# A hash-masked attention and MLP kernel: score banks, spare slots for exponentials, one way of hashing, weights in two transfers, and a new order

## The chip, the cores and the metric

The kernel runs on one core of a Trainium2 chip. The metric is the device time of one execution in microseconds (us). Three runs of the kernel before took 304.24 to 305.08 us, with a median of 304.82. A profile of one more execution (303.7 us) shows what each engine did; the profiled span, from the first to the last instruction of the program, is 302.0 us.

Engines: TensorE (PE; PEld is its loading of weights), VectorE (DVE), ScalarE (ACT), GpSimd (POOL) and SyncE (SP). SP's queue issues most DMAs, POOL's queue those that convert fp32 to bf16 on the way.

## The reference

The kernel computes attention in which a query sees only keys of its own hash bucket, and then a layer norm and an MLP with a residual. Shapes: q, k, v are (4, 8, 768, 64): 4 batches, 8 heads, 768 positions, 64 dimensions; proj is (64, 6); w_ch1 is (512, 2048) and w_ch2 (2048, 512); the result is (4, 768, 512).

```python
q_bits = (np.einsum('bhsd,dk->bhsk', q, proj) > 0)
k_bits = (np.einsum('bhsd,dk->bhsk', k, proj) > 0)
mask = q_bucket[:, :, :, None] == k_bucket[:, :, None, :]
scores = np.where(mask, 0.125 * np.matmul(q, k.transpose(0, 1, 3, 2)), -1e9)
attn = softmax(scores)
x = np.matmul(attn, v)                      # heads side by side: (4, 768, 512)
xn = (x - mean(x)) / sqrt(var(x) + 1e-6) * g_ln
out = x + relu(xn @ w_ch1) @ w_ch2
```

(The lines are shortened: the bucket is the number that the six bits form.)

## The kernel before

**Units and steps.** The 768 positions of each of 4 batches are cut into 3 blocks of 256 queries, so there are 12 units u. The 8 heads are two groups g of four heads. For a unit and a group, the 768 keys are taken in three parts kp of 256. So there are 72 steps s = 6u + 3g + kp, and each has three parts:

- S (line 516): 24 products. For each of two blocks of 128 keys and four heads, one product of the hash bits and two of the halves of the 64 dimensions add up in PSUM. Equal hashes add a constant that the exponential's bias takes away again; unequal ones end so far below that the exponential is 0.
- E (line 522): two exponentials on ScalarE, two heads each (128 x 1024 elements), from the score banks into an SBUF tile E.
- A (line 541): 16 products of E with the values v, with a column of ones that gives the denominator, into the accumulator `acc` of the unit and group.

After the three steps of a group come `na` and `nb` (the division, DVE), `nc` (statistics) and, after both groups, `ce` (mean away, times g_ln). The result is transposed (`ft`, `fc` with TensorE for unit 0, `fl` by DMA for the others). The MLP's first product is F (line 598): 8 pieces p for each unit, each 8 products over 256 columns of w1. R is its relu (DVE, line 608, or ACT, line 606). D (line 614) is the second product, Z (line 622) the residual, O the output DMA.

**Score banks.** PSUM has the tags scA, scB and acc, each of two banks, and f1, f2. The two halves of a step's scores go to scA and scB. For the steps named in `ROT` they rotate over scA, scB and acc instead, as `acc` holds nothing yet; A's accumulator has the tag acc, so the first A waits for the last exponential that reads scores from there.

**SBUF slots.** `SLOTS` gives each tile of a tag its buffer by hand. E has four buffers, `hb` (the relu's result) two, `x` (a unit's attention result) four.

**Batch 0's hash.** q and k of batch 0 come in pieces of 256 positions: `lx` (line 338) loads, `tn` (DVE, line 270) transposes twice, `ca` (lines 277 to 281) casts to bf16. The hash of a piece goes one of two ways. The full product: `ha` (line 359) is four fp32 products with the projection spread over all 128 columns (`pfull`), and `bh` (line 273) compares with 0 on DVE into the bit tile G. The compact way: `hc` (line 370) is 16 small products with `p32`, `bc` compares, `sl` (line 383) is four products with a matrix `spread` that brings the bits to their place, and `bi` (lines 393 to 395) copies them to G, on DVE or ACT. `sel` makes `spread` on POOL. Eight pieces go the first way and four the second. The other batches are loaded as a whole (`LX`, after a marker `gx` in the first column), transposed with `tu`, cast with `CA`, hashed with `hm` and spread by way of DRAM (`mw`, `mr`).

**Weights.** `lw1` loads a quarter of w1 (512 columns: F's pieces 2n and 2n+1), `lw2` a quarter of w2, `lg` (line 398) g_ln, copied to all partitions (`gB`). `lv` loads v (batch 0 in two loads of four heads), `cv` (POOL, line 417) casts it, `sq` and `sc` make its sum over keys. `wm` (line 331) are products that nothing reads; they keep TensorE busy at the start.

**Order.** `ORDER` is a hand-given list of operations, read once: a word is the operation, the engine (v DVE, a ACT, p POOL, s SP, t TensorE) and its arguments. Each engine does its own words in this order, and waits where data or a buffer isn't ready; so S.t.6.2 is step 6's S, F.t.0.1 unit 0's piece 1, and E.a.5.1 the second half of step 5's exponentials. The first steps come in the order 0, 1, 2, 4, 3, 5, 8, 6, 7, 9, 10.

Of the kernel before, what the change touches and what calls it, by code (L numbers as in the profile page):

```python
# [38 lines left out]
tu.v.1.1.0.0 A.t.12.2 E.a.13.1 LX.s.2.0.0 S.t.16.2 E.a.16.0 E.a.16.1 A.t.13.2 tu.v.1.1.1.3 tu.v.1.1.0.1 tu.v.1.1.0.3 rs.p.0
D.t.0.0.2 D.t.0.0.3 mr.s.1.0.1 cv.p.1.4.0 Z.v.0.0 tu.v.1.1.1.1 CA.p.1.1.1 cv.p.1.4.2 S.t.15.2 lv.s.1.0.2 cv.p.1.0.0 E.a.15.0  # L40
mr.s.1.0.2 mr.s.1.0.3 hm.t.1.1 E.a.15.1 D.t.0.1.0 CA.a.1.1.0 S.t.17.2 E.a.17.1 mr.s.1.0.0 bt.v.1.1 mw.s.1.1 mr.s.1.1.3
na.v.2.0 nb.v.2.0 F.t.1.2 R.v.1.2 su.p.1.0 A.t.15.2 E.a.17.0 cv.p.1.0.2 A.t.16.2 F.t.1.6 S.t.18.2 R.a.1.6
nc.v.2.0 F.t.1.5 R.v.1.5 D.t.0.1.1 mr.s.1.1.2 E.a.18.0 A.t.17.2 E.a.18.1 sp.t.1.0 sc.v.1.0 na.v.2.1 S.t.20.2
# [637 lines left out]
```

## Time and profile before

| what | time or share |
|---|---|
| runs | 304.24, 304.82, 305.08 us |
| profiled execution | 303.7 us, of it the span 302.0 us |
| F, 768 products (line 598) | 99.3 us busy, mean 273 ns |
| S, 1728 products (line 516) | 52.4 and 42.6 us busy |
| A, 1152 products (line 541) | 46.2 us busy |
| E, 144 exponentials (line 522) | 153.5 us busy, mean 1111 ns |
| first E begins | 10.00 us |
| first F begins on the chain of waits | 35.46 us |
| TensorE's last product ends | 298.3 us |
| DMA read and written | 28.12 MB and 6.88 MB |

Products on TensorE overlap, so busy times of single products are longer than the steps from one to the next; the chain of waits gives the latter (F's 8 products: 0.87 us; A's 16: 0.49; S's 24: 0.77 to 0.83). In the chain each row is a start, a duration, and the engine and line that the program's end hung on at that time. In a timeline a row is one or several instructions of one kind, with the idle time ahead of them in square brackets.

### The profile page before, as it was taken

What the parts mean: (1) busy time and instruction counts of PE and PEld (TensorE: products, weight loads), DVE (VectorE), ACT (ScalarE), POOL (GpSimd) and SP (SyncE); (2) the same over time, 40 slices, a digit from 0 to 9 for tenths busy, and PEclk for the clock granted to TensorE, in tenths of its full rate; (3) what the DMA queues carried; (4) which work ended last, traced back from release to release, by engine and by line L of the source; (5) the groups of instructions that cost most, each with busy time, mean ns of one, the idle gap of its engine ahead of it and who ended that gap; (6) DMA issues with size and microseconds to landing.
All of it is one profiled execution on the core that took longest, in us unless ns stands there. A gap on an engine that the chain in (4) does not pass through costs nothing.

```text
span 302.0 us, 9823 instructions
## 1 busy us (share of the span) xinstructions
PE 290.5 (96%) x4345; PEld 202.5 (67%) x4394; DVE 175.9 (58%) x364; ACT 189.0 (63%) x206; POOL 76.4 (25%) x103
## 2 busy tenths in 40 slices
PE   8988899999999999999999999999999999999995
PEld 4666677676766767677666776667666776676663
DVE  4878758759767564875749466274554346443322
ACT  2587888778646777777667866854565665643010
POOL 5497062476017101300750002700101001001000
PEclk9999999999999999999999999999999999999999
DMA  6999999718768453420322242012201501003132
GB/s 221 310 299 247 282 212 270 177 35 230 201 159 246 84 217 95 98 72 18 80 66 41 68 100 51 21 35 54 54 2 35 106 2 37 20 2 89 52 87 71
DMA packets 31194, 34.32 MB, mean 114 GB/s; under 512 B 15536, under 2 KB 27824, under 8 KB 31152
## 3 DMA queue, kind: packets, MB, share of 16 engines
q1 hardware_dynamic: 26080, 28.98, 35.0%
q0 software_dynamic: 4224, 4.19, 8.5%
q8 instruction: 34, 0.56, 0.8%
q10 hardware_dynamic: 848, 0.53, 0.7%
q14 instruction: 8, 0.07, 0.1%
HBM read 28.12 MB, written 6.88 MB: 116 GB/s over the span
## 4 chain that ended last, share of the span: by engine, by line
PE 94%; ACT 3%; issue 1%; DVE 0%
PE f L598 29%; PE sc L516 19%; PE acc L541 12%; PE hp L471 3%; ACT E L522 3%; PE hf L359 2%; PE warm L328 1%; PE f_110None L614 1%; PE f_101None L614 1%; PE f L614 1%; PE f_90None L614 1%; PE f_20None L614 1%; PE f_80None L614 1%; PE f_21None L614 1%; PE f_00None L614 1%
## 5 line engine op out<-in xcount | busy, mean ns | idle before, releaser
L522 ACT ACTIVATE E<-sc,bias_sb 128x1024 bf16<-128x1024 f32 x144 | 153.5, 1111 | 60.6 <-PE sc L516 60.6
L598 PE MATMUL f<-xnT,w_sb 128*128 128x256 bf16 x768 | 99.3, 273 | 0.1
L598 PEld LDWEIGHTS <-w_sb 128*128 128x128 bf16 x768 | 70.8, 98 | 22.6 <-issue 7.4
L608 DVE TENSOR_SCALAR hb<-f 128x512 bf16<-128x512 f32 x49 | 33.7, 690 | 59.2 <-PE f L598 58.8
L614 PEld LDWEIGHTS <-hb 128*128 128x128 bf16 x400 | 36.0, 98 | 31.2 <-issue 3.0
L516 PE MATMUL sc<-qb,kb 32*128 32x256 bf16 x1152 | 52.4, 267 | 0.0
L606 ACT ACTIVATE hb<-f 128x512 bf16<-128x512 f32 x47 | 28.0, 596 | 35.9 <-PE f L598 35.9
L541 PEld LDWEIGHTS <-E 128*128 128x128 bf16 x1152 | 42.7, 98 | 8.2 <-issue 3.2
L541 PE MATMUL acc<-vaug,E 128*128 128x65 bf16 x1152 | 46.2, 194 | 0.1
L516 PE MATMUL sc<-G 6*128 6x256 bf16 (+1 forms) x576 | 42.6, 273 | 2.7 <-ACT E L522 2.0
L576 POOL TENSOR_SCALAR rs<-mv 128x2 f32<-128x2 f32 x12 | 7.7, 640 | 106.9 <-DVE mv L570 106.6
L516 PEld LDWEIGHTS <-kb 32*128 32x128 bf16 x1152 | 30.4, 93 | 1.5
L516 PEld LDWEIGHTS <-G 6*128 6x128 bf16 (+1 forms) x576 | 15.7, 91 | 20.7 <-issue 17.4
L417 POOL CAST vaug<-vn 128x768 bf16<-128x768 f32 x16 | 14.0, 884 | 58.3 <-DMA vn<-in_v_dram 44.2
L270 DVE STREAM_TRANSPOSE T<-X 128x384 f32<-128x384 f32 (+2 forms) x52 | 26.8, 542 | 1.2 <-DMA X<-in_k_dram 1.2
L554 DVE SCALAR_TENSOR_TENSOR y<-vsB,acc 128x520 f32<-128x520 f32 x24 | 16.5, 688 | 10.5 <-PE acc L541 10.2
L571 DVE SCALAR_TENSOR_TENSOR xc<-x,mv,gB 128x512 bf16<-128x512 f32 x24 | 18.6, 775 | 0.9
L567 DVE BATCH_NORM_STATS2 st<-x 128x6 f32<-128x256 f32 x48 | 17.7, 412 | 0.3
L563 DVE TENSOR_TENSOR x<-y,rc 128x512 f32<-128x512 f32 x24 | 16.8, 699 | 0.8
L425 POOL TENSOR_TENSOR t<-vn 128x768 f32<-128x768 f32 x6 | 10.9, 1812 | 0.0
L281 POOL CAST kb<-T 128x1536 bf16<-128x1536 f32 x3 | 4.4, 1461 | 22.3 <-DVE T L270 22.3
L270 DVE STREAM_TRANSPOSE tp<-X 128x256 f32<-128x256 f32 x24 | 9.0, 416 | 1.4 <-DMA X<-in_q_dram 0.9
(113 smaller groups left out, 236.7 us busy)
## 6 DMA issues: line engine op xcount, KB each, us to landing
out_dram<-x SPq DMA_DIRECT2D x45, 128.0 KB, 2.0
X<-in_k_dram SPq DMA_DIRECT2D x7, 768.0 KB, 5.8
X<-in_q_dram SPq DMA_DIRECT2D x6, 768.0 KB, 4.7
vn<-in_v_dram SPq DMA_DIRECT2D x24, 192.0 KB, 6.0
w_sb<-in_moe_w_ch_dram POOLq DMA_DIRECT2D x8, 512.0 KB, 15.9
vn<-in_v_dram SPq DMA_DIRECT2D x2, 768.0 KB
X<-in_q_dram SPq DMA_DIRECT2D x2, 512.0 KB, 12.2
Bd<-B SPq DMA_DIRECT2D x6, 96.0 KB, 2.5
```

Of the source, the lines that this page charges most:

```text
L270: nc.vector.transpose(d[:, j], s[:, j, kj0 : kj0 + n])
L516: nc.tensor.matmul(sc(s, i // 2)[:, i % 2, 256 * kk : 256 * kk + 256], lh, rh, start=(rep == 0), stop=(rep == 2), skip_group_check=True,)
L522: nc.scalar.activation(E(s)[:, heads(h)], sc(s, h), AF.Exp, scale=EXP_SCALE, bias=bias_sb)
L541: nc.tensor.matmul(acc[:, qt, (D + 1) * i : (D + 1) * (i + 1)], E(s)[:, i, 256 * kk + P * qt : 256 * kk + P * qt + P], vaug(u // 3)[:, 4 * ...
L554: nc.vector.scalar_tensor_tensor(yt(u, g), vs, EPS_ROW, made[f"acc{u}{g}"][:, :, :A], op0=AOP.mult, op1=AOP.add,)
L563: nc.vector.tensor_tensor(xo, a[:, :, :, 0:D], rc.to_broadcast([P, 2, 4, D]), op=AOP.mult)
L567: nc.vector.bn_stats(stats(u)[:, qt, g], xt(u)[:, qt, 256 * g : 256 * g + 256])
L571: nc.vector.scalar_tensor_tensor(xc(u)[:, t], xt(u)[:, t], mv(u)[:, t, 0:1], gB, op0=AOP.subtract, op1=AOP.mult,)
L598: nc.tensor.matmul(f1[:, n].rearrange("p (t x) -> p t x", t=2), w1_sb[:, dt, P * nt : P * nt + P], xnT(u)[:, :, dt], start=(dt == 0), stop ...
L606: nc.scalar.activation(hb(u)[:, 2 * p : 2 * p + 2], f1, AF.Relu)
L608: eng.tensor_scalar_max(hb(u)[:, 2 * p : 2 * p + 2], f1, 0.0)
L614: nc.tensor.matmul(f2, hb(u)[:, nt, P * t : P * t + P], w2_sb[:, nt, half(h)], start=(nt == 0), stop=(nt == NNT - 1),)
```

## The change

Five edits come together. `ROT` names six steps instead of three, so the scores of steps 4, 3 and 5 rotate over three bank pairs too. The E tiles of the first four of these steps take the slots of hb (steps 0 and 1) and x (2 and 4). `sel`, `hc`, `Bc`, `bc`, `sl` and `bi` are gone, and all twelve pieces of batch 0 are hashed by `ha` and `bh`. `lw1` loads half of w1 (1024 columns: F's pieces 0 to 3 or 4 to 7), so there are two of them. The order is a new one: three `wm` instead of eight, `lg` second on SP's queue, three casts of queries on DVE, and, up to the first F, this:

```diff
-ROT = (0, 1, 2)
+ROT = (0, 1, 2, 4, 3, 5)
 ORDER = """
-mem.v lp.a lx.a.0.1.0.1 tab.a pf.v lx.s.0.0.0.1 warm.t wm.t.0 wm.t.1 wm.t.2 wm.t.3 sel.p
-tn.v.0.0.0 p32.p tn.v.0.1.0 ca.p.0.1.0 lx.s.0.1.1.3 ha.t.0.0.0 wm.t.4 lx.s.1.1.0.3 lx.s.1.0.0.1 ha.t.0.1.0 lv.s.0.0.4 ca.a.0.0.0
-lx.s.0.0.1.3 bh.v.0.0.0 wm.t.5 tn.v.0.1.1 ha.t.0.1.1 lw2.p.1 bh.v.0.1.0 ca.p.0.1.1 S.t.0.2 lv.s.0.4.4 E.a.0.0 E.a.0.1
-tn.v.0.1.2 tn.v.1.1.1 ca.p.1.1.1 lx.s.1.0.1.3 wm.t.6 wm.t.7 bh.v.0.1.1 ha.t.1.1.1 on.p.0 bh.v.1.1.1 tn.v.1.1.0 S.t.1.2
-E.a.1.0 ca.v.0.1.2 gx.p.1.0.0 ha.t.0.1.2 bh.v.0.1.2 E.a.1.1 tn.v.1.0.0 ca.p.1.0.0 ca.v.1.1.0 ha.t.1.1.0 bh.v.1.1.0 tn.v.1.1.2
-S.t.2.2 E.a.2.0 cv.p.0.0.0 ha.t.1.0.0 bh.v.1.0.0 S.t.4.2 cv.p.0.0.2 tn.v.0.0.1 hc.t.0.0.1 ca.p.0.0.1 lw1.p.3 bc.v.0.0.1
-gx.p.1.0.1 ha.t.1.1.2 LX.s.1.0.0 tn.v.0.0.2 E.a.2.1 E.a.4.0 LX.s.1.0.1 E.a.4.1 bh.v.1.1.2 sl.t.0.0.1 bi.v.0.0.1 cv.p.0.4.2
-A.t.0.2 S.t.3.2 A.t.1.2 ca.v.1.1.2 lg.s lw1.p.1 sq.t.0.0 E.a.3.0 A.t.2.2 sc.v.0.0 E.a.3.1 S.t.5.2
-E.a.5.0 cv.p.0.4.0 sq.t.0.4 na.v.0.0 nb.v.0.0 lw1.p.2 lw1.p.0 nc.v.0.0 E.a.5.1 S.t.8.2 sc.a.0.4 A.t.5.2
-E.a.8.0 E.a.8.1 tu.v.1.0.0.2 lw2.p.0 tn.v.1.0.1 A.t.4.2 ca.p.1.0.1 hc.t.0.0.2 tn.v.1.0.2 A.t.3.2 tu.v.1.0.1.0 bc.v.0.0.2
-lw2.p.3 gx.p.1.1.1 tu.v.1.0.0.1 sl.t.0.0.2 na.v.0.1 bi.a.0.0.2 S.t.6.2 E.a.6.0 LX.s.1.1.1 E.a.6.1 hc.t.1.0.1 nb.v.0.1
-hc.t.1.0.2 bc.v.1.0.2 sl.t.1.0.2 bi.a.1.0.2 bc.v.1.0.1 pmem.p S.t.7.2 A.t.8.2 E.a.7.0 lv.s.1.4.1 nc.v.0.1 ce.v.0.1
-ce.v.0.0 ft.t.0.1 lv.s.1.4.2 E.a.7.1 fc.a.0.1 sl.t.1.0.1 tu.v.1.0.1.1 bi.v.1.0.1 A.t.6.2 ft.t.0.0 S.t.9.2 E.a.9.0
-on.p.1 lw2.p.2 fc.v.0.0 E.a.9.1 F.t.0.6 F.t.0.7 tu.v.1.0.1.2 R.a.0.6 A.t.7.2 tu.v.1.0.0.0 S.t.10.2 R.v.0.7
-na.v.1.0 nb.v.1.0 lv.s.1.4.0 tu.v.1.0.0.3 tu.v.1.0.1.3 E.a.10.0 CA.p.1.0.1 F.t.0.3 F.t.0.4 E.a.10.1 A.t.9.2 ca.a.0.0.2
...
-O.s.10.0 R.v.11.2 D.t.11.0.0 F.t.11.5 R.a.11.5 O.s.10.2 D.t.11.0.1 F.t.11.7 O.s.10.3 D.t.11.0.2 R.v.11.7 D.t.11.0.3
-D.t.11.1.0.0 D.t.11.1.1.0 D.t.11.1.2.0 O.s.8.2 D.t.11.1.3.0 D.t.11.1.0.1 D.t.11.1.1.1 rs.p.11 Z.v.11.0 O.a.11.0.0 O.s.11.0.1 Z.v.11.1.0
-O.a.11.1.0.0 O.s.11.1.1.0 D.t.11.1.2.1 D.t.11.1.3.1 Z.v.11.1.1 O.s.11.1.1.1 O.a.11.1.0.1
+mem.v lp.a lx.a.0.1.0.1 tab.a pf.v pmem.p warm.t on.p.0 wm.t.0 lx.s.0.0.0.1 lg.s tn.v.0.0.0
+tn.v.0.1.0 ha.t.0.0.0 lx.s.0.1.1.3 bh.v.0.0.0 ha.t.0.1.0 lx.s.1.1.0.3 bh.v.0.1.0 ca.a.0.0.0 wm.t.1 wm.t.2 lx.s.1.0.0.1 tn.v.0.1.1
+ca.a.0.1.0 S.t.0.2 p32.p tn.v.0.1.2 on.p.1 ha.t.0.1.1 E.a.0.0 bh.v.0.1.1 tn.v.1.1.1 ha.t.0.1.2 ca.p.0.1.1 S.t.1.2
+gx.p.1.0.0 bh.v.0.1.2 tn.v.1.0.0 lx.s.0.0.1.3 E.a.0.1 ca.p.0.1.2 ca.p.1.1.1 lv.s.0.0.4 cv.p.0.0.0 E.a.1.0 cv.p.0.0.2 tn.v.1.1.0
+ha.t.1.1.1 bh.v.1.1.1 ca.v.1.1.0 S.t.2.2 lx.s.1.0.1.3 ca.v.1.0.0 ha.t.1.0.0 tn.v.0.0.1 E.a.1.1 E.a.2.0 lv.s.0.4.4 bh.v.1.0.0
+ha.t.1.1.0 tn.v.1.1.2 cv.p.0.4.2 bh.v.1.1.0 lw2.p.2 E.a.2.1 S.t.4.2 E.a.4.0 ha.t.1.1.2 E.a.4.1 S.t.3.2 E.a.3.0
+tn.v.0.0.2 ha.t.0.0.1 ca.v.1.1.2 gx.v.1.0.1 cv.p.0.4.0 tn.v.1.0.2 bh.v.1.1.2 ca.v.0.0.1 S.t.5.2 bh.v.0.0.1 ca.v.0.0.2 E.a.3.1
+tn.v.1.0.1 sq.t.0.0 sc.v.0.0 E.a.5.0 S.t.8.2 E.a.5.1 A.t.0.2 A.t.2.2 ca.p.1.0.2 E.a.8.0 LX.s.1.0.0 tu.v.1.0.0.1
+tu.v.1.0.0.2 gx.p.1.1.1 lv.s.1.4.0 A.t.1.2 na.v.0.0 sq.t.0.4 nb.v.0.0 nc.v.0.0 E.a.8.1 S.t.6.2 A.t.5.2 A.t.3.2
+A.t.4.2 sc.a.0.4 E.a.6.0 E.a.6.1 LX.s.1.0.1 tu.v.1.0.1.2 na.v.0.1 nb.v.0.1 lv.s.1.4.2 nc.v.0.1 lw1.p.1 ha.t.1.0.1
+S.t.7.2 E.a.7.0 bh.v.1.0.1 ha.t.1.0.2 bh.v.1.0.2 lv.s.1.4.3 ha.t.0.0.2 lv.s.1.0.3 ca.p.1.0.1 lw1.p.0 lw2.p.0 tu.v.1.0.0.3
+E.a.7.1 S.t.9.2 E.a.9.0 A.t.7.2 ce.v.0.1 bh.v.0.0.2 A.t.8.2 E.a.9.1 gx.v.1.1.0 lw2.p.1 ce.v.0.0 ft.t.0.0
+fc.v.0.0 A.t.6.2 na.v.1.0 tu.v.1.0.1.3 ft.t.0.1 LX.s.1.1.0 fc.a.0.1 rs.p.0 tu.v.1.0.1.0 S.t.10.2 E.a.10.0 tu.v.1.0.1.1
+F.t.0.6 tu.v.1.0.0.0 CA.p.1.0.0 A.t.9.2 LX.s.1.1.1 CA.v.1.0.1 E.a.10.1 R.a.0.6 F.t.0.7 S.t.11.2 E.a.11.0 E.a.11.1
+A.t.10.2 R.v.0.7 F.t.0.1 lv.s.1.0.2 R.v.0.1 F.t.0.4 R.a.0.4 S.t.14.2 E.a.14.0 F.t.0.3 lv.s.1.0.0 E.a.14.1
...
+R.a.11.5 O.s.9.1 O.s.10.2 rs.p.11 D.t.11.1.1.0 F.t.11.6 R.a.11.6 O.s.9.0 D.t.11.0.2 O.s.10.0 D.t.11.0.3 Z.v.11.0
+O.a.11.0.0 D.t.11.1.2.0 O.s.11.0.1 D.t.11.1.3.0 D.t.11.1.0.1 Z.v.11.1.0 O.a.11.1.0.0 O.s.11.1.1.0 D.t.11.1.1.1 D.t.11.1.2.1 D.t.11.1.3.1 Z.v.11.1.1
+O.a.11.1.0.1 O.s.10.3 O.s.11.1.1.1
 SLOTS = dict(
-    Bc="0120",
-    E="012301213021301230132031230120313210302103230123021320120302130212310230",
+    E="01231012301203123013210321020301230123031203123031210320123012031231",
...
-    X="0123021302310210",
-    hb="010101010101",
+    X="0123021320310230",
+    hb="01010101010101",
...
-    x="012301230123",
+    x="01230132013201",
...
     def E(s):
-        return sb(f"E{s}", [P, 4, 512], BF16, "E", 4)
+        tag, bufs = (("hb", 2), ("hb", 2), ("x", 4), ("x", 4))[ROT.index(s)] if s in ROT[:4] else ("E", 4)
+        return sb(f"{'E' if tag == 'E' else 'E' + tag[0]}{s}", [P, 4, 512], BF16, tag, bufs)
...
-    def sel(eng):
...
-    def hc(eng, g, t, kp):
...
-    def bc(eng, g, t, kp):
...
-    def sl(eng, g, t, kp):
...
-    def bi(eng, g, t, kp):
...
     def lw1(eng, n):
-        nc.gpsimd.dma_start(out=w1_sb[:, :, 512 * n : 512 * n + 512], in_=w1ap[:, :, 512 * n : 512 * n + 512])
+        nc.gpsimd.dma_start(out=w1_sb[:, :, 1024 * n : 1024 * n + 1024], in_=w1ap[:, :, 1024 * n : 1024 * n + 1024])
```

In the middle of the order, left out here, the same F, D, S and A of the later units are interleaved in another sequence.

More of the change, by code (lines that the diff above doesn't have):

```diff
@@ L39 @@
[L39 to L43, printed above, removed]
@@ new lines @@
+D.t.6.1.0 S.t.58.2 nb.v.8.1 nc.v.8.1 ce.v.8.1 F.t.7.4 E.a.58.0 su.p.3.4 R.a.7.4 E.a.58.1 ce.v.8.0 A.t.56.2
+D.t.6.1.1 fl.s.8.1 sp.t.3.4 sc.v.3.4 D.t.6.1.2 sp.t.3.0 sc.a.3.0 S.t.59.2 E.a.59.1 E.a.59.0 F.t.7.5 R.v.7.5
+A.t.55.2 D.t.6.1.3 Z.v.6.1 cv.p.3.4.2 F.t.7.3 O.s.5.2 R.v.7.3 S.t.60.2 E.a.60.0 E.a.60.1 O.s.5.0 na.v.9.0
+fl.s.8.0 D.t.7.0.0 F.t.8.5 R.a.8.5 nb.v.9.0 nc.v.9.0 A.t.58.2 S.t.61.2 F.t.7.6 E.a.61.0 A.t.57.2 R.a.7.6
+A.t.59.2 rs.p.8 F.t.8.3 na.v.9.1 O.s.6.0 E.a.61.1 R.v.8.3 S.t.64.2 E.a.64.0 E.a.64.1 D.t.7.0.1 O.s.6.1
@@ L297, in pmem @@
         )
-    def sel(eng):
-        nc.gpsimd.memset(spread, 0.0)
-        for c in range(CC):
-            nc.gpsimd.affine_select(
-                out=spread[:, c].rearrange("p (i b) -> p i b", b=32)[:, :, :NB],
-                in_=ones.rearrange("p (i b) -> p i b", b=32)[:, :, :NB],
-                pattern=[[-8, 4], [-1, NB]], base=-32 * c, channel_multiplier=1, compare_op=AOP.is_equal, fill=0.0,
-            )
     def tab(eng):
@@ L640 @@
     OPS = dict(
-        mem=mem, pmem=pmem, tab=tab, lp=lp, sel=sel, pf=pf, p32=p32c, warm=warm, wm=wm, lx=lx, tn=tn, ca=ca, ha=ha, bh=bh, hc=hc, bc=bc, sl=sl, bi=bi, lg=lg,
+        mem=mem, pmem=pmem, tab=tab, lp=lp, pf=pf, p32=p32c, warm=warm, wm=wm, lx=lx, tn=tn, ca=ca, ha=ha, bh=bh, lg=lg,
         lw1=lw1, lw2=lw2, on=on, lv=lv, cv=cv, su=su, sp=sp, sq=sq, sc=scp, LX=LX, gx=gx, tu=tu, CA=CA, hm=hm, bt=bt, mw=mw, mr=mr,
```

163 lines of the change are left out of this document (70 added, 93 removed).

## Prediction

> **What bounds the kernel now.** I read the page's busy shares first, then the busy times of six stretches, then the chain of waits up to 50 us, then VectorE (DVE), GpSimd (POOL) and SyncE (SP) in order of time.
>
> ```profile
> PE 290.5 (96%) x4345; PEld 202.5 (67%) x4394; DVE 175.9 (58%) x364; ACT 189.0 (63%) x206; POOL 76.4 (25%) x103
> ...
> 8.50:20.34 11.84, 11.26 (x185) 7.78 (x183) 9.86 (x26) 8.47 (x8) 8.14 (x12) 1.00 1.09 335
> 20.34:35.46 15.12, 12.57 (x313) 9.73 (x314) 12.00 (x31) 12.02 (x15) 8.12 (x14) 1.00 1.07 246
> 35.46:60.45 24.99, 24.63 (x450) 17.85 (x454) 16.70 (x35) 20.93 (x23) 9.58 (x8) 1.00 1.01 224
> 60.45:294.76 234.31, 231.15 (x3350) 160.96 (x3396) 131.23 (x252) 145.42 (x159) 46.04 (x55) 1.00 0.32 79
> ```
>
> The columns are the stretch, its length, then busy us of PE, PEld, DVE, ACT, POOL, the granted clock, DMA share and GB/s. From the first F (35.46) on TensorE is busy 98 to 99% of the time: whatever is still to be done then is done at its pace. Time can be won ahead of 35.46, where its work waits, and after its last matmul (298.3). So what counts is how much product work is done by the time the first F starts.
>
> ```profile
> 19.32 1.02 PE sc L516 x24
> 20.35 2.12 ACT E L522 x2
> 22.51 0.84 PE sc L516 x22
> 23.36 2.12 ACT E L522 x2
> 25.52 0.83 PE sc L516 x22
> ...
> 29.51 2.13 ACT E L522 x2
> 31.68 0.83 PE sc L516 x22
> ...
> 34.44 1.02 PE sc L516 x24
> 35.46 1.85 PE f L598 x16
> ```
>
> From 19 us the path alternates: 24 score products (S, 0.83), then two exponentials (E, 2.12), then the next S, which needs the bank pair that E has just read. That is a step every 3.0 us, though ScalarE needs 2.12. The three-bank rotation covers only steps 0, 1, 2.
>
> ```profile
> 13.57 0.76 DVE L270 STREAM_TRANSPOSE tp<-X 128x256 f32<-128x256 f32 x2
> 14.26 0.60 DVE L281 CAST kb<-tp 128x512 bf16<-128x512 f32 x1
> 14.79 0.41 DVE L273 TENSOR_SCALAR G<-hf 128x256 bf16<-128x256 f32 x1
> ...
> 19.43 1.18 DVE L281 CAST kb<-tp 128x512 bf16<-128x512 f32 x1
> ...
> 20.05 1.24 POOL L417 CAST vaug<-vn 128x768 bf16<-128x768 f32 x1
> ...
> 20.54 2.00 SPq L398 DMA_DIRECT2D gB<-in_moe_g_ln_dram  x1
> ```
>
> DVE feeds the early steps: a pair of transposes each 0.69 us after the one before (0.77 busy, overlapped), a hash comparison 0.35, a key cast 0.53. The last two rows are a cast and a load that the change moves or doubles.
>
> **The change, part by part.** I follow the new order on each engine with these durations.
>
> *Head.* Five of eight single warm-up products (L331) go; three of the first four (0.43 each) stand ahead of the first hash product, which ends at 7.04 now. It can start at 5.05 instead, partly at the slow rate of the warm-up (0.86 warm, 1.72 at half rate; I take 1.3). Both first hash products are then done at 7.15, step 0's S starts at 7.6 and its E at 8.5 instead of 10.00: 1.5 us earlier. SP issues gB (2.00) second, ahead of five X pieces and both v loads. Its 256 KB cost the keys between 0.8 (335 GB/s) and 2.0 (the issue); at the 232 GB/s of the first 8.5 us it is 1.1, and I take that: the last keys land near 10.2.
>
> *Hash by full products.* Four hc+sl pairs (0.36 + 0.12) become four ha (0.86): 4 x 0.38 = 1.5 us more TensorE work, all of it before the first F, where ScalarE's 2.12 a step covers it; uncovered it costs the 1.5. On DVE bc + bi (0.23 + 0.41) becomes one comparison (0.42). POOL loses `sel` (0.53 + 0.83), which nothing waits for. DVE makes five of batch 0's casts instead of three, three of them of queries: no row has that at this size; it lies between 0.32 (a third of the 0.96 of a 128x1536 one) and 0.62 (a key cast), or 1.18 where a POOL cast runs beside it. I take 0.5.
>
> *Third bank pair, E in hb and x slots.* With DVE's chain the E start at 8.5, 11.1, 13.2, 16.3 (step 4 waits for its query hash on DVE; 17.33 now), 18.4, 20.5, 22.65 (step 8; 26.35 now). From step 6 on the pairs alternate again, 3.1 each: 25.75, 28.95, 32.0, the last being step 9, done at 34.1; now step 7 ends at 34.58. A (the E-times-v products) start only when the accumulator bank is free of scores, at 22.65 instead of 18.84, and the second group's end near 27.2 instead of 28.4. The longer life of the first E costs nothing, as hb and x are first written after 24 us. Then the normalization (7.0 us from A to F now: 28.4 to 35.4) gives the transposed x at 34.4, step 10's S follows, and F starts at 35.25. Gain: 0.2 on the start, and one S (0.77) and one A (0.50) more are done by then: 1.27. Together 1.5.
>
> *Weights.* w1 comes in two transfers of 1024 columns. The third F (F.0.1, at 38.8) now needs the second of them; before, the quarter that it reads was used only at 47. Before, four quarters issued from 19.2 on; the last, issued at 23.5, landed 17.2 us later, at 40.7. Alone on the queues a 512 KB piece takes 2.5 us (212 GB/s between 40.7 and 45.7). Five pieces' worth (a quarter of w2 goes ahead) from 20.7 on is 12.4 us, and 1.5 MB of X and v in between is 3.9 at the 400 GB/s of 16 to 20 us: 37.0. Two more X loads, issued near 32, add up to 3.9: 41. So its wait lies between 0 and 2.2 us; those X loads need some 3.9 us from issue to first packet (20.16 to 24.06 for the same load now), so I take 38.5, no wait.
>
> [...]
>
> *Order anew.* Counting neighbours on TensorE after the first F and pricing each pair of kinds by its mean in this trace (an F after an A costs 0.97, after a D 0.91; an A after an F 0.61, after a D 0.51), the new order is 0.3 us cheaper, beside the S and A already counted. *Tail:* SP issues one more output (O.10.3) between the last two pieces, one issue of 0.44; 0.3 us later, between 0 and 0.5.
>
> **Sum:** -1.5 - 0.3 + 0.3 = -1.5. The profiled execution took 303.7 (span 302.0 and 1.7 around it), so 302.2; the median of the runs is 304.82, 1.1 above it, so **303.3**. Own bounds 302.2 to 304.2: the start of step 4 by 0.9 either way (casts at 0.32 or 0.62, gB at 0.8 or 2.0).
>
> **Rivals.**
> *The second half of w1 is late* (the slower side). F.0.1 stands on TensorE and holds F.0.4, S 14 and all behind them: with its landing at 41 to 43 the wait is 2.2 to 4.2, so 305.5 to 307.5. For it: four pieces needed 21.5 us from first issue to last landing, and from 35 us on X loads run beside the weights as before. Against: gB is out of the way and POOL issues the two as early as 23 and 25. It decides from a landing of 38.8 on.
> *DVE sets the pace of the first steps.* The banks are free but the hash comes late, from gB ahead of the keys (0.9 more) and casts at 1.18 (0.6 more each, two or three of five meeting POOL's four v casts). F starts 1.2 to 2.7 later: 304.5 to 306.0, the gain gone. For it: DVE is busy 9.86 of 11.84 us from 8.5 on. Against: from step 3 on it has 0.7 to 1.9 us in hand in my walk.
> [...]
> *More than I count.* No cost of gB, casts at 0.32, no tail: 301.7 to 302.2.
>
> **How the numbers follow.** A measurement of this kernel tells 0.3% (0.9 us) from no change: faster is under 303.9, slower over 305.7. The forecast has 0.50 (0.45 faster, 0.05 same), the weights 0.26 (0.25 slower, 0.01 same), DVE 0.16 (0.09 same, 0.07 slower), more gain 0.08 (faster): faster 0.53, same 0.15, slower 0.32. The range runs from 302.0 to 306.8; the likeliest case's own is 302.2 to 304.2.
>
> **What would show it.** Right: first E near 8.5, step 8's near 22.7, no idle ScalarE between steps 4, 3, 5, 8; first F within 0.5 us of 35.3 with eleven S and nine A ahead of it; TensorE waiting for no DMA. Wrong: TensorE idle ahead of F.0.1 until a w landing (the weights); E of step 4 after 17.3, or DVE casts over 1 us (DVE's pace); X from k landing after 11; idle TensorE after 60 us, which would be a fault of the new order that I have priced at nothing.

## The result, and the profile after

The changed kernel takes 310.12 us (median of six runs, 307.55 to 313.04) against 304.78 for the kernel before in the same measurement (304.24 to 305.08). Two of the six, 312.51 and 313.04, count as slow runs and are left out of the ratio; the other four have a median of 308.08. The ratio is 1.0136, with an interval of 1.0099 to 1.0174. It is slower by 1.4%, where 303.3 was forecast, in a range of 302.0 to 306.8. All six runs after spread over 5.5 us, those before over 0.8. The profiled execution took 308.59 us, with a span of 306.8.

The page's busy shares after, and the busy times of the stretches that were shown of before:

```profile
PE 292.9 (95%) x4279; PEld 202.8 (66%) x4325; DVE 175.5 (57%) x363; ACT 185.7 (61%) x204; POOL 83.3 (27%) x95
```

```profile
0.00:8.50 8.50, 5.18 (x14) 2.23 (x14) 2.81 (x17) 2.12 (x3) 1.97 (x14) 1.00 0.63 202
8.50:20.34 11.84, 11.48 (x123) 7.23 (x124) 9.21 (x25) 7.60 (x8) 5.88 (x8) 0.86 1.03 353
20.34:35.46 15.12, 14.09 (x250) 10.29 (x251) 12.35 (x30) 12.39 (x13) 7.85 (x9) 1.00 1.01 211
35.46:60.45 24.99, 23.83 (x455) 17.64 (x454) 19.21 (x39) 19.10 (x23) 11.85 (x8) 1.00 0.97 240
60.45:294.76 234.31, 230.56 (x3386) 160.48 (x3429) 130.19 (x252) 143.32 (x158) 55.80 (x57) 1.00 0.32 77
```

From 60 us on little has changed: TensorE is busy 230.56 us of it against 231.15, and one F waits 0.7 us for a transposed load. The loss lies ahead. Two numbers of the second row must be read together: TensorE is busy 11.48 us, more than before, but runs 123 products instead of 185 (of those missing, 20 are the compact hash's and 19 are A, which the new order has later), at a granted clock of 0.86. Busy is not fast. The head shows why, in VectorE's rows, TensorE's and SyncE's (start, duration, the idle time ahead in brackets). First the row of the first key piece before, then the rows after:

```profile
4.97 0.77 DVE L270 STREAM_TRANSPOSE tp<-X 128x256 f32<-128x256 f32 x2 [0.17 <-DMA X<-in_k_dram]
```

```profile
4.25 0.77 DVE L268 STREAM_TRANSPOSE tp<-X 128x256 f32<-128x256 f32 x2 [1.08 <-DMA X<-in_q_dram]
7.92 0.77 DVE L268 STREAM_TRANSPOSE tp<-X 128x256 f32<-128x256 f32 x2 [2.90 <-DMA X<-in_k_dram]
...
8.42 1.68 PE L348 MATMUL hf<-tp,pfull 128*128 128x256 f32 x4 [2.21 <-DVE tp L268]
...
1.57 0.59 SPq L357 DMA_DIRECT2D gB<-in_moe_g_ln_dram  x1
```

The first key piece is transposed at 7.92 instead of 4.97. TensorE idles 2.21 us for it and then takes 1.68 us for four products that take 1.13 at full clock (at 14.97 of the same trace): between 8.42 and 12.30 the granted clock is 0.56. From 4 to 5 and from 5 to 6 us, when the key piece should land and the next ones follow, the queues move 169 and 158 GB/s, where before they moved 350 and 325 (the last column; before, then after):

```profile
4.00:5.00 1.00, 1.00 (x4) 0.36 (x3) 0.80 (x3) 0.17 (x1) 0.00 (x0) 1.00 1.12 350
5.00:6.00 1.00, 1.00 (x4) 0.43 (x3) 0.74 (x2) 0.46 (x1) 0.12 (x1) 1.00 1.04 325
```

```profile
4.00:5.00 1.00, 1.00 (x4) 0.40 (x3) 0.75 (x2) 0.00 (x0) 0.00 (x0) 1.00 0.63 169
5.00:6.00 1.00, 1.00 (x5) 0.70 (x4) 0.02 (x1) 0.63 (x1) 0.00 (x0) 1.00 0.67 158
```

gB, issued at 1.57, is the only transfer that is new there. In the DMA records its 128 packets run from 3.82 to 7.32 us. The key piece's last packet ends at 7.38 (4.41 before), although its load was issued earlier, at 1.22, on ScalarE's queue.

ScalarE's rows, the first F's surroundings on TensorE, and the piece of w1 on the chain of waits:

```profile
12.39 2.12 ACT L481 ACTIVATE Eh<-sc,bias_sb 128x1024 bf16<-128x1024 f32 x2 [2.58 <-PE sc L475]
15.08 2.12 ACT L481 ACTIVATE Eh<-sc,bias_sb 128x1024 bf16<-128x1024 f32 x2 [0.57 <-PE sc L475]
17.09 2.12 ACT L481 ACTIVATE Ex<-sc,bias_sb 128x1024 bf16<-128x1024 f32 x2
20.07 2.12 ACT L481 ACTIVATE Ex<-sc,bias_sb 128x1024 bf16<-128x1024 f32 x2 [0.87 <-PE sc L475]
22.12 6.13 ACT L481 ACTIVATE E<-sc,bias_sb 128x1024 bf16<-128x1024 f32 x6
...
33.48 2.12 ACT L481 ACTIVATE E<-sc,bias_sb 128x1024 bf16<-128x1024 f32 x2 [1.96 <-PE sc L475]
```

```profile
32.55 0.29 PE L475 MATMUL sc<-G 32*128 32x256 bf16 x4 [0.67 <-issue]
44.07 1.92 PE L557 MATMUL f<-xnT,w_sb 128*128 128x256 bf16 x16 [0.79 <-DMA w_sb<-in_moe_w_ch_dram]
```

```profile
24.98 1.45 POOL qb L277
26.43 17.59 DMA w_sb<-in_moe_w_ch_dram
```

The third bank pair works: one row holds six exponentials (three steps) without a gap, and step 8 is done at 28.25 although the first E began at 12.39, 2.4 us later than before. S of step 7 waits 0.67 us for nothing that the profile names ("issue"). The half of w1 that F.0.1 reads was issued at 26.43 and takes 17.6 us to come. It holds F.0.1 by only 0.79 us here, because everything ahead of it is four microseconds late too.

So the first F starts at 39.50, and the products end at 302.5 instead of 298.3.

### The profile page after: what moved, and what is told of

The parts are those of the page before. It is cut to its first block, busy times and chain, and to the rows that moved or that the text cites. A ratio compares the mean times of both kernels' runs of the same rounds, so it can differ in the third digit from the quotient of the medians.

```text
span 306.8 us, 9669 instructions
## 1 busy us (share of the span) xinstructions
PE 292.9 (95%) x4279; PEld 202.8 (66%) x4325; DVE 175.5 (57%) x363; ACT 185.7 (61%) x204; POOL 83.3 (27%) x95
## 4 chain that ended last, share of the span: by engine, by line
PE 82%; DMA 7%; DVE 2%; issue 1%; POOL 0%; SPq 0%
PE f L557 28%; PE sc L475 15%; PE acc L500 10%; DMA w_sb<-in_moe_w_ch_dram 6%; PE hp L430 2%; DMA xnT<-xc 1%; PE f_50None L573 1%; PE f_100None L573 1%; PE f L573 1%; PE f_101None L573 1%; PE f_81None L573 1%; PE f_71None L573 1%; PE f_41None L573 1%; PE f_31None L573 1%; PE f_11None L573 1%
## 5 line engine op out<-in xcount | busy, mean ns | idle before, releaser
L481 ACT ACTIVATE E<-sc,bias_sb 128x1024 bf16<-128x1024 f32 x136 | 145.0, 1111 | 63.3 <-PE sc L475 63.3
L567 DVE TENSOR_SCALAR hb<-f 128x512 bf16<-128x512 f32 x47 | 32.3, 688 | 60.2 <-PE f L557 60.0
L565 ACT ACTIVATE hb<-f 128x512 bf16<-128x512 f32 x49 | 29.1, 595 | 37.4 <-PE f L557 37.1
L500 PEld LDWEIGHTS <-E 128*128 128x128 bf16 x1088 | 39.3, 98 | 6.1 <-issue 4.1
L500 PE MATMUL acc<-vaug,E 128*128 128x65 bf16 x1088 | 42.7, 194 | 0.1
L277 POOL TENSOR_SCALAR qb<-T 128x1536 bf16<-128x1536 f32 x4 | 17.0, 4251 | 40.7 <-DVE T L268 40.7
L513 DVE SCALAR_TENSOR_TENSOR y<-vsB,acc 128x520 f32<-128x520 f32 x24 | 16.5, 687 | 18.4 <-PE acc L500 17.6
L348 PE MATMUL hf<-tp,pfull 128*128 128x256 f32 x48 | 13.4, 416 | 2.4 <-DVE tp L268 2.2
L376 POOL CAST vaug<-vn 128x768 bf16<-128x768 f32 x16 | 13.3, 841 | 7.0 <-DMA vn<-in_v_dram 7.0
L384 POOL TENSOR_TENSOR t<-vn 128x768 f32<-128x768 f32 x6 | 11.8, 1960 | 12.0 <-DMA vn<-in_v_dram 12.0
```

What stands on the lines that cost most here:

```text
L277: eng.tensor_scalar(dst, src, QS, None, op0=AOP.mult)
L481: nc.scalar.activation(E(s)[:, heads(h)], sc(s, h), AF.Exp, scale=EXP_SCALE, bias=bias_sb)
L500: nc.tensor.matmul(acc[:, qt, (D + 1) * i : (D + 1) * (i + 1)], E(s)[:, i, 256 * kk + P * qt : 256 * kk + P * qt + P], vaug(u // 3)[:, 4 * ...
L565: nc.scalar.activation(hb(u)[:, 2 * p : 2 * p + 2], f1, AF.Relu)
L567: eng.tensor_scalar_max(hb(u)[:, 2 * p : 2 * p + 2], f1, 0.0)
```

## The experiments

Each kernel ran beside the kernel before on the same chip; "before" had medians of 304.16 to 304.80 in these measurements. A weight's landing is the last update of its transfer's semaphore; packets come from the trace's DMA records. In the diffs a line is a part of the order.

### gB and the weights, each by itself

**e1_gb_late**: gB goes back behind the first X load of batch 1.

```diff
-wm.t.0 lx.s.0.0.0.1 lg.s tn.v.0.0.0
+wm.t.0 lx.s.0.0.0.1 tn.v.0.0.0
...
-E.a.8.0 LX.s.1.0.0 tu.v.1.0.0.1
+E.a.8.0 LX.s.1.0.0 lg.s tu.v.1.0.0.1
```

> The changed kernel with the load of gB (lg) moved from second place on SP's queue to behind the first load of batch 1 (LX.1.0.0). Theory: the early gB is the cause. Its 256 KB hold back the first key piece from 4.9 to 7.9 us, TensorE runs out of work for 2.2 us and then at half rate for 3.4 us, and the first F starts at 39.5 instead of 35.3. Then here: the second pair of transposes near 5.0, granted clock 1.000, first E at 8.5 to 9.0, first F at 35.5 to 36.5, and 303 to 304.5 us with a spread of the runs under 0.5%. Rival: the second half of w1, which lands at 43.9 in the changed kernel, is the real bound; then F.0.1 starts at 42 to 43.5 whatever the head does, and the time falls by only 1 to 2 us, to 306 to 307.5.

310.89 us (309.31 to 312.83), ratio 1.0227 [1.0193, 1.0260]. The head comes as forecast: first E 8.22, step 8's at 21.6, first F 35.7. But then TensorE's waits, and the stretch that follows:

```profile
PE f L557 <- DMA w_sb<-in_moe_w_ch_dram: 6.3, 2, 5.7
```

```profile
42.00:49.50 7.50, 4.28 (x36) 2.87 (x40) 2.28 (x5) 0.60 (x1) 2.25 (x3) 0.54 1.20 237
```

The columns of the first are the total, the number of waits and the longest. F.0.1 waits 5.7 us, as its half of w1 lands at 45.18, and the clock is half for 6.8 us. Everything won at the head is lost here, and more: the time is beyond the rival's 306 to 307.5, the ratio above the changed kernel's 1.0136. With the head on time the weights are the whole loss against the kernel before (e6 below, with both moved, is level with it).

**e2_before_gb_early**: the kernel before with gB second on SyncE, and nothing else.

```diff
-lx.s.0.0.0.1 warm.t wm.t.0
+lx.s.0.0.0.1 lg.s warm.t wm.t.0
...
-ca.v.1.1.2 lg.s lw1.p.1
+ca.v.1.1.2 lw1.p.1
```

> The kernel before with one word moved: gB's load second on SP's queue, as in the changed one. Theory that gB is the cause: the second pair of transposes waits until near 7.9 us (4.97 now), the first E comes at 11 to 12.5 (10.00 now), and the time rises by 1.5 to 3 us, to 306 to 308. Rival (the head's lateness is made good before the first F, and the rest of the change costs the time): within 0.5 us of 304.8.

305.79 us, ratio 1.0057 [1.0038, 1.0077]; the span is 1.6 us longer, and the first key piece comes at the same time as in the changed kernel:

```profile
7.88 0.77 DVE L270 STREAM_TRANSPOSE tp<-X 128x256 f32<-128x256 f32 x2 [2.80 <-DMA X<-in_k_dram]
```

TensorE idles 1.84 us there and keeps its full clock in this profile.

**e3_warm**: ten more warm-up products behind the first hash product of the changed kernel.

```diff
-ha.t.0.0.0 lx.s.0.1.1.3
+ha.t.0.0.0 wm.t.10 wm.t.11 wm.t.12 wm.t.13 wm.t.14 wm.t.15 wm.t.16 wm.t.17 wm.t.18 wm.t.19 lx.s.0.1.1.3
```

> The changed kernel with ten more products that nothing reads (wm) behind the first hash product, some 2.2 us at full rate: TensorE has work while it waits for the late key piece, and the piece is as late as before. Theory that the half clock after the wait is a part of the loss: granted clock 1.000, the first E at 11.0 to 11.5 instead of 12.39, runs within 0.5% of each other instead of 1.8%, and 1 to 2 us less than the changed kernel's 310.1 (or its fastest, 307.6). Rival, the clock is no part of it: first E at 12 to 12.5, same time and same spread.

308.12 us (306.82 to 309.64), ratio 1.0130 [1.0102, 1.0158], against 1.0136 for the changed kernel: the same. The profiled execution has the full clock at the head:

```profile
8.00:12.00 4.00, 3.91 (x39) 2.58 (x38) 2.21 (x7) 1.99 (x2) 1.08 (x3) 1.00 1.06 369
```

Its first E comes at 11.11, 1.3 us earlier than in the changed kernel. But the first F comes at 39.74, against 39.50, and the profiled span is the same 306.8 us. A wait that the profile calls "issue" takes the gain back; it is followed up below.

```profile
31.51 0.36 PE L500 MATMUL acc<-vaug,Ex 128*128 128x65 bf16 x6 [1.48 <-issue]
```

So the half clock costs 1.3 us at the first E. That it is a part of the loss at the end is not shown.

**e4_gb_late_quarters**: e1 with w1 in quarters again, in the order 3, 0, 2, 1.

```diff
-lw1.p.1 ha.t.1.0.1
+lw1.p.3 lw1.p.0 ha.t.1.0.1
...
-lw1.p.0 lw2.p.0
+lw1.p.2 lw1.p.1 lw2.p.0
```

> As the run with gB late, and w1 again in four quarters of 512 columns, issued in the order in which the F use them (3, 0, 2, 1), two each where the halves stood. Theory that the halves are late: F.0.1 needs only two quarters and doesn't wait, so that this is 1 to 3 us under the run with gB late, 302.5 to 303.5. Rival, the halves cost nothing once the head is right: within 0.5 us of that run.

310.58 us, ratio 1.0204 [1.0177, 1.0230]. The wait only moves: F.0.3 stands 4.1 us for the last quarter, which lands at 45.98. The size of the pieces is not the cause.

**e5_quarters_w2_later** (e4) and **e6_halves_w2_later** (e1): the quarter of w2 that stood first on GpSimd's queue goes behind w1 and two other quarters of w2. **e7_gb_early_w2_later** is the changed kernel with that edit alone.

```diff
-bh.v.1.1.0 lw2.p.2 E.a.2.1
+bh.v.1.1.0 lw1.p.1 E.a.2.1
...
-lw1.p.1 ha.t.1.0.1
+lw1.p.0 ha.t.1.0.1
...
-ca.p.1.0.1 lw1.p.0 lw2.p.0
+ca.p.1.0.1 lw2.p.0
...
-lw2.p.1 ce.v.0.0
+lw2.p.1 lw2.p.2 ce.v.0.0
```

> gB late, w1 in quarters, and the quarter of w2 that stands first on POOL's queue (lw2.2) behind the w1 quarters and two others of w2. With gB late alone, TensorE waited 5.7 us at F.0.1 for the second half of w1 (landed 45.1); with quarters 4.1 us at F.0.3 (quarter 1 landed 45.7). Theory: w1 lands too late because a w2 quarter goes ahead of it and because it starts only at 24 us, so that two X loads (36 to 42 us) catch its last piece. Then here the w1 quarters land one place earlier (30, 32.5, 35 and 40 us), F waits under 1 us in all, granted clock 1.000, first F at 35.7, and 302.5 to 304 us. Rival: the weights aren't all; idle TensorE after 60 us or the last pieces of w2 take the gain, 305 to 307.

> The same with w1 in halves, as the change has it. The second half would land near 40 us, F.0.1 needs it at 39.0: a wait of 0 to 2 us. Theory that the halves themselves cost little: within 1 us of the run with quarters. Rival, the halves are the fault (four pieces' worth needed for the third F): 2 to 4 us above the run with quarters, with a cold clock.

> The changed kernel with lw2.2 behind w1 as its only edit: gB is second on SP's queue again. The first F comes at 39.5 as in the changed kernel, and w1's second half has landed by then. If the head alone is left, this is the first F's lateness of 3.8 us above the run with halves and gB late: 306 to 307.5, TensorE waiting for no w. Rival, that the weights' place is worth nothing in the presence of the late head: 308 to 310 as the changed kernel.

| kernel | median us | ratio to before | first F | w1's two halves (e5: last quarter) land |
|---|---|---|---|---|
| after | 308.08 (four runs) | 1.0136 [1.0099, 1.0174] | 39.50 | 36.99, 44.02 |
| e5 | 306.13 | 1.0043 [1.0027, 1.0059] | 36.46 | 40.12 |
| e6 | 304.91 | 1.0016 [0.9999, 1.0033] | 36.43 | 33.06, 39.03 |
| e7 | 306.28 | 1.0049 [1.0034, 1.0064] | 38.25 | 34.74, 40.19 |

In all three no F waits for a weight. With gB early the place of that quarter is worth 0.9%, some 2.7 us, by the ratios (1.0136 to 1.0049; by the medians of the table 1.8), and with gB late 6.0 us (e1 to e6). With the quarter in its new place gB is worth another 1.4 (306.28 to 304.91). Halves are no worse than quarters. But e6 only equals the kernel before, and e5 is in its rival's range; the 1.5 us that the forecast saw as a gain are still missing. Its two largest waits from 8 us on:

```profile
PE sc L475 <- issue: 1.3, 1, 1.3
...
PE f_00None L573 <- DMA w_sb<-in_moe_w_ch_dram: 0.9, 1, 0.9
```

**e8_three_steps**: e6 with the third bank pair for the first three steps only.

```diff
-"acc")[(2 * ROT.index(s) + h) % 3] if s in ROT else
+"acc")[(2 * ROT.index(s) + h) % 3] if s in ROT[:3] else
```

> The run with halves and gB late, with the score banks rotating only in the first three steps, as before the change (the E tiles stay in their idle slots, the order is the same). Theory that the third pair is worth what the chain showed: steps 4, 3, 5 and 8 come 3.0 us apart instead of 2.0, the first F 2 to 3 us later, and the time rises by 2 to 3 us. Rival: hashing or the weights bound the first F; under 0.7 us.

305.34 us, ratio 1.0031 [1.0018, 1.0045]: 0.4 above e6, although the first F comes 1.7 us later (38.08) and S waits 2.5 us for E. Less at the end than at the first F. Both kernels have the wait named "issue" at about the same length (1.41 and 1.34), so it is not what makes the difference small.

### The hash by full products

**e9_before_full_products**: the kernel before with its four compact pieces done by full products.

```diff
-hc.t.0.0.1 ca.p.0.0.1 lw1.p.3 bc.v.0.0.1
+ha.t.0.0.1 ca.p.0.0.1 lw1.p.3
...
-sl.t.0.0.1 bi.v.0.0.1
+bh.v.0.0.1
```

(and the same for 0.0.2, 1.0.2 and 1.0.1)

> The kernel before with one part of the change alone: the four hash pieces of batch 0 that went by the compact product, the copy, the select and the add go by full products as the other pieces do. Theory (the prediction's step: this is covered): the first F stays within 0.4 us of the 35.4 us of before and the time within 0.4 us of before. Rival (TensorE's own added products stand on the path): first F about 1.5 us later, time +1.0 to +1.6 us, 305.8 to 306.4.

306.61 us (305.61 to 309.45), ratio 1.0083 [1.0053, 1.0113]: near the rival's numbers and a little beyond them. The first F comes at 37.5. Part of it is not the products but VectorE, where the comparisons now stand in front of the normalization:

```profile
30.40 1.99 PE L359 MATMUL hf<-tp,pfull 128*128 128x256 f32 x8 [0.56 <-DVE G L273]
34.66 0.40 PE L585 MATMUL ft<-ident,xc 128*128 128x128 bf16 x4 [0.91 <-DVE xc L571]
36.42 0.38 PE L585 MATMUL ft<-ident,xc 128*128 128x128 bf16 x4 [0.87 <-DVE G L273]
```

**e13_compact_hash**: e6 with the compact hash put back (`sel`, `hc`, `bc`, `sl`, `bi` as before), at the places of the full products.

```diff
-tn.v.0.0.2 ha.t.0.0.1 ca.v.1.1.2
+tn.v.0.0.2 hc.t.0.0.1 bc.v.0.0.1 ca.v.1.1.2
...
-S.t.5.2 bh.v.0.0.1
+sl.t.0.0.1 S.t.5.2 bi.v.0.0.1
```

(and so for the other three)

> The kernel e6_halves_w2_later with one part of the change undone: the four hash pieces of batch 0 go by the compact product, the comparison, the four selecting products and the copy again, at the places that their full products have in the new order, with the table of the selecting products built on GpSimd as before. On the order of before the full products alone cost 1.8 us by medians and 2.1 us at the first F. Theory A (their 1.5 us of TensorE work stand on the path in the new order too, since the third bank pair leaves no waits for ScalarE there): first F at 34.9 to 35.5 instead of 36.4, time 303.4 to 304.2. Theory B (the prediction's: in the new order they are covered, and e9 lost the time only to VectorE's order): first F within 0.4 us of 36.4 or later, time 304.6 to 305.4.

308.59 us, ratio 1.0124 [1.0085, 1.0163]; neither theory. The compact way goes twice over VectorE, and in an order made for the full products the selecting products wait:

```profile
32.88 0.28 PE L383 MATMUL hf<-Bc,spread 128*128 128x64 bf16 x4 [3.02 <-DVE Bc L273]
```

It tells that the two parts of the change belong together, not what the 1.5 us of products cost in the new order.

### The wait before S of step 7

In seven kernels with the new order the wait named "issue" sits at the same instruction. This table has the end of the second 16-KB packet of the instruction queue (q8 on the page: 34 packets, 0.56 MB), the start of S of step 7 and the idle time ahead of it:

| kernel | packet ends | S of step 7 | waited |
|---|---|---|---|
| after | 31.15 | 32.55 | 0.67 |
| e1 | 26.19 | 27.72 | 0.32 |
| e4 | 27.39 | 28.69 | 1.01 |
| e5 | 28.19 | 29.50 | 1.66 |
| e6 | 28.18 | 29.48 | 1.34 |
| e7 | 29.80 | 31.30 | 1.48 |
| e8 | 29.64 | 31.12 | 1.41 |

The work starts again 1.30 to 1.53 us after the packet. In all seven, 351 products of the trace stand ahead of the wait. In e3, with ten more products in front, the wait moved ahead in the work, to an A at 31.51, 1.46 us after its packet (30.06), and again 351 products stand ahead of it. So in these eight traces it stands at one place in the instruction stream, not at step 7. In the kernel before that packet ended at 22.16, and TensorE came to its 352nd product 5.8 us later.

**e10_values_later**: e6 with four early transfers of batch 1's values behind the last X piece, to leave the queues room. **e11_values_later_w2_together** adds the last quarter of w2 right behind the third.

```diff
-gx.p.1.1.1 lv.s.1.4.0 A.t.1.2
+gx.p.1.1.1 A.t.1.2
...
-LX.s.1.1.1 CA.v.1.0.1
+LX.s.1.1.1 lv.s.1.4.0 lv.s.1.4.2 lv.s.1.4.3 lv.s.1.0.3 CA.v.1.0.1
```

> The kernel e6_halves_w2_later with one edit: the four transfers of batch 1's values that SyncE issued from 17.9 to 28 us (192 KB each, not used before 48 us) are issued behind the last X piece of batch 1 (LX.1.1.1). In all runs with the new order the wait before S of step 7 ended 1.3 to 1.5 us after a 16-KB packet of the instruction queue, and that packet started about 5 us later than TensorE's instruction count at which it started in before. Theory (the instruction block waits behind SyncE's transfers, which hold all 16 DMA engines from 18 to 25 us): with 768 KB less there, about 3.5 us of all engines, the packet ends at 22 to 25 us instead of 28.2, the 1.3 us wait labelled issue before S of step 7 is gone or under 0.4 us, the first F starts at 34.8 to 35.4 instead of 36.4 and the time falls by 0.6 to 1.5 us, to 303.4 to 304.3. Rival (the wait belongs to the order of the work or to the place of the block, not to the transfers): the wait stays at 1.0 us or more, first F within 0.4 us of 36.4, time 304.6 to 305.2.

> The kernel e10_values_later with one more edit: the last quarter of w2 is issued right behind the third instead of behind GpSimd's copy of batch 1's queries (4.7 us of work at 38 us). Theory: it lands by about 54 us or before instead of 56.9, and the 0.9 us that the first D waits for it goes: 0.5 to 1.0 us below e10. Rival (the transfers of X and values then fall together with the weights and the wait goes to another F, D or S): within 0.4 us of e10.

e10: 307.55 us, ratio 1.0097 [1.0069, 1.0126]. The head does what the theory says: packet at 25.28, no wait before S of step 7, first F 34.20. The end does not: GpSimd's sum of the values comes late, and the clock is half for 3.4 us behind it.

```profile
PE vp L391 <- POOL vsum L386: 3.5, 1, 3.5
```

e11: 308.12 us, ratio 1.0102 [1.0081, 1.0123], with 4.0 us at the same place; the packet ends at 27.56 and 0.9 us of the wait is back. The last quarter of w2 could not be judged there.

**e12_later_half_of_values** moves only the second half of the values, ahead of `lv.s.1.4.1`; **e14_both** adds e13's edits.

> The kernel e6_halves_w2_later with the three early transfers of the second half of batch 1's values (lv.1.4.0, .2, .3, 576 KB) issued directly ahead of the fourth (lv.1.4.1); the first half stays where it is. In e10 all four late transfers stood ahead of pieces that GpSimd sums first, and TensorE waited 3.5 us for that sum at 56 us. Theory (the wait before S of step 7 comes from the instruction block behind SyncE's transfers; the values only have to come in the order in which they are used): that wait is under 0.4 us, the first F starts 34.8 to 35.6 instead of 36.4, no wait for the sum over 0.5 us, time 303.4 to 304.3. Rival 1 (transfers of this stretch are short of rate in any order): the wait for the sum is 1 us or more, 305.5 to 307. Rival 2 (the wait before S is not of the transfers): it stays at 1 us or more, 304.6 to 305.3.

> Both edits of e12_later_half_of_values and e13_compact_hash on e6_halves_w2_later: the third bank pair and the new order with the compact hash, gB late, w1 ahead of w2 and the values of batch 1's second half late. If both theories hold (the instruction block and the 1.5 us of products), first F 34.0 to 34.6 and time 302.6 to 303.6, below before's 304.8 by more than its spread. If the gains overlap (the path after S of step 7 is ScalarE's or VectorE's), 303.4 to 304.2. Rival (waits move to the weights of the first F and D): 304.5 to 305.5.

316.83 us (ratio 1.0394 [1.0353, 1.0435]) and 320.40 (1.0512 [1.0484, 1.0539]), far outside of every expectation. At the head e12 is near what the theory says (wait 0.52, where under 0.4 was expected; first F 35.34). But the two halves of the values now ask for their two staging slots in swapped order, a value transfer of batch 2 waits on SyncE for GpSimd to be done with its slot, from 74 to 87 us, and the transposes queued behind it hold F:

```profile
87.49 0.35 SPq L373 DMA_DIRECT2D vn<-in_v_dram  x1
87.95 1.19 SPq L539 DMA_TRANSPOSE xnT<-xc  x1
...
90.83 1.86 PE L557 MATMUL f<-xnT,w_sb 128*128 128x256 bf16 x8 [8.46 <-DMA xnT<-xc]
```

**e15_three_values_behind** and **e16_two_values_behind**: the same on e6 with the slots kept, three or two transfers directly behind `lv.s.1.0.1`.

```diff
-lv.s.1.0.1 E.a.12.0
+lv.s.1.0.1 lv.s.1.4.2 lv.s.1.4.3 E.a.12.0
```

> The kernel e6_halves_w2_later with three of the four early transfers of batch 1's values (lv.1.4.0, .2, .3; 576 KB) issued behind the last one of the first half (lv.1.0.1) instead of from 17.9 us on, the staging slots kept as they were. In e12 they stood further back, the two halves swapped their staging slots, and a later value transfer waited 14 us on SyncE's queue ahead of the transposes that the F steps need; this edit keeps them clear of both. Theory (S of step 7 waits for the instruction block, which comes earlier when SyncE's transfers leave room): wait before S of step 7 under 0.6 us, first F 34.2 to 35.5 instead of 36.4, no wait over 1 us for the value sum or for the transposes, time 302.9 to 304.2, at or below the kernel before. Rival (the traffic between 35 and 60 us has no room for 576 KB more): waits of 1 us or more for the value sum, the transposes or the weights, 305 to 307.

> As e15_three_values_behind with two transfers (lv.1.4.2 and .3, 384 KB) moved instead of three. Theory: the wait before S of step 7 is between those of e6 (1.3) and e15, first F 34.6 to 36.0, time 303.2 to 304.6. Rival: as in e15, by two thirds: 304.8 to 306.

e15: 304.70 us, ratio 1.0013 [0.9995, 1.0030], between theory and rival; 0.94 us of the wait stay (packet at 27.54), and the transposes cost 1.9. e16: **303.41 us** (302.82 to 304.48, twelve runs), ratio 0.9965 [0.9952, 0.9979], faster than both kernels. No wait before S of step 7, and from 8 to 36 us no wait of TensorE above 0.25 us. In ScalarE's rows of e16 step 7 follows step 6 by 3.35 us and step 9 by 3.1 more, where e6 had 4.75 ahead of step 7 (first row e6's step 7, then e16's steps 6, 7 and 9):

```profile
30.41 2.12 ACT L481 ACTIVATE E<-sc,bias_sb 128x1024 bf16<-128x1024 f32 x2 [2.64 <-PE sc L475]
```

```profile
26.31 2.12 ACT L481 ACTIVATE E<-sc,bias_sb 128x1024 bf16<-128x1024 f32 x2 [0.39 <-PE sc L475]
29.66 2.12 ACT L481 ACTIVATE E<-sc,bias_sb 128x1024 bf16<-128x1024 f32 x2 [1.23 <-PE sc L475]
32.77 2.12 ACT L481 ACTIVATE E<-sc,bias_sb 128x1024 bf16<-128x1024 f32 x2 [1.00 <-PE sc L475]
```

Why the packet comes when it does is open. Counted from each kernel's first E it started 18.0 us after it in e6, 16.2 to 17.8 in e10, e12, e15 and e16, but 16.5 also in e1, where no value transfer had moved, and 19.1 in e17 below, which has e16's transfers. Fewer transfers do not explain it alone.

**e17_three_steps_again**: e16 with e8's edit.

> The kernel e16_two_values_behind with the third bank pair only in the first three steps, as e8 did it to e6. In e6 the wait before S of step 7 (1.3 us) could hide part of what the pair gives, 0.4 us by medians and 1.7 us at the first F in e8; in e16 that wait is gone. Theory (the pair's gain reaches the end once nothing waits behind it): 1.0 to 2.0 us above e16, 304.4 to 305.4. Rival (the E steps behind step 8 and ScalarE's later work take the gain back in any case): 0.2 to 0.7 us above e16, 303.6 to 304.1.

306.57 us (305.01 to 307.49), ratio 1.0072 [1.0051, 1.0093], 3.2 above e16 and beyond the theory's range. S waits for E again:

```profile
17.64 0.28 PE L475 MATMUL sc<-G 32*128 32x256 bf16 x2 [0.72 <-ACT Ex L481]
20.59 0.28 PE L475 MATMUL sc<-G 32*128 32x256 bf16 x2 [0.72 <-ACT E L481]
23.53 0.28 PE L475 MATMUL sc<-G 32*128 32x256 bf16 x2 [0.72 <-ACT E L481]
```

Its profile shows 1.0 us more span and a first F 1.1 us later, from a first E that is 1.25 us earlier: 2.3 us for the pair. Counted the same way, from the first E to the first F, it is 2.7 us in e8 (30.19 us, against 27.47 in e6). So the profiles of both pairs of kernels agree on the head. Why the medians are 0.4 us apart in one pair and 3.2 in the other, no run shows.

## Why the prediction was wrong

Right were the direction of reading (everything is decided ahead of the first F, nothing after 60 us) and the walk of the steps. Taken from the first E, the forecast's starts and the profile's are:

| | step 0 | 4 | 3 | 8 | 6 | 7 | 9 | first F |
|---|---|---|---|---|---|---|---|---|
| forecast | 8.5 | 16.3 | 18.4 | 22.65 | 25.75 | 28.95 | 32.0 | 35.25 |
| after, less 3.89 | 8.5 | 16.18 | 18.23 | 22.23 | 25.51 | 29.59 | 32.53 | 35.61 |

Eleven S and nine A stand ahead of the first F, as said. The kernel is what was described, only 3.9 us later, and with a wait behind it.

**Head: the step that failed first.** It priced gB as 256 KB added at the queues' rate, 0.8 to 2.0 us on the last keys. What it holds is the first key piece, by 3.0 us (7.92 for 4.97), and from 4 to 6 us the queues move half as much (169 and 158 GB/s, for 350 and 325). The key piece's last packet ends 0.04 to 0.06 us after gB's last one in all three kernels with the early gB (7.32 and 7.38 in the changed kernel, 7.28 and 7.32 in e2, 7.06 and 7.12 in e7). TensorE has nothing else to do, and in the changed kernel the clock is halved on top, 1.3 us at the first E (e3). The first E came at 12.39, not 8.5; with gB late it came at 7.9 to 9.3. By itself gB costs 1.6 us on the order of before (e2) and 1.4 on the new one (e7 against e6).

**Weights: the step that failed most.** "So I take 38.5, no wait" was worked out from rates; the landing was 44.02, and 45.18 in e1. The rival had the mechanism and 2.2 to 4.2 us for landings of 41 to 43; the wait was 5.7 in e1, beyond the rival's end, and with it came 6.8 us at half clock, which no term held. The sum lets five pieces run from 20.7 on, be through at 37.0 and so escape the X loads. In e1 the first weight was issued at 19.73, but its first packet went at 23.82. When the X loads' first packets came, at 35.8, some 2.1 of the 2.5 MB were through, and the weights' rate fell from some 200 KB a microsecond to 80. So the start was mis-sized by 3.1 us, enough for the missing 0.4 MB at the full rate, and the choice that the X loads come too late fell with it. Moving the quarter of w2 out of the way was worth 2.7 us by the ratios with gB early (e7) and 6.0 with gB late (e6).

In the changed kernel both failures overlap, so that neither shows alone: the late head hides the late weights (0.79 us of wait), and mending the head alone (e1) brings no gain: its ratio is 1.0227, against 1.0136.

**Hash by full products.** "ScalarE's 2.12 a step covers it" fell on the order of before, where the products cost 1.8 us (e9), its uncovered price and a little more. In the new order it is not shown apart. It was argued against itself: the third bank pair takes away those waits of TensorE that were to hide the products. In e16 TensorE is busy 33.78 of the first 36 us, against 31.76 before, which leaves little room to cover them; that is argued, not shown.

**Third bank pair.** The term (1.5 with what follows from it) was not too large at the first F: 2.3 us in e17 and 2.7 in e8. At the end it is 0.4 us by the medians of e8 and 3.2 by those of e17, so its size there stays open. VectorE's pace, a rival, did not come: query casts took 0.41 to 0.77 us on VectorE in the changed kernel, around the 0.5 taken. One key cast took 1.28, a sign that the prediction had named for this rival, yet the walk held to 0.4 us up to step 8.

**Instruction block.** No step had the wait that goes with it: 0.67 us in the changed kernel, and in e6 1.34. e16, without that wait, is 1.5 us below e6 by the medians.

**Order and tail.** From the first F to the last product it is 263.0 us (302.5 - 39.5) against 262.8 before, and 261.5 without the two waits for transfers (0.79 and 0.7). The forecast had 261.2 (1.27 and 0.3 less), so both terms hold to 0.3. The end behind the last residual was 3.36 us before (298.64 to 302.0) and is 3.89 now: 0.5, the upper bound, where 0.3 was taken. (The forecast's own bounds, 0.9 either way of 303.3, begin at 302.4 and not at 302.2.)

With the three orders mended (gB, w2's quarter, two value transfers), the change gives 303.41, close to the 303.3 that was forecast for it. That is luck and no credit to the forecast: e16 is another kernel than the one forecast, and it still carries 0.9 us of a late transpose and the full products, which the sum had at nothing. How its gain divides among the parts is not shown.
